# Fewer K, Q, V buffers, and the order of transposes, masks and states, in a fused retention and hard-swish MLP kernel

## The chip, the cores and the metric

The kernel runs on one core of a Trainium2 chip. The metric is the device time of one execution in microseconds (us); the time of a kernel is the median of its runs. Engines are named as the profile names them: PE is TensorE's matrix multiplication and PEld its weight load, DVE is VectorE, ACT is ScalarE, POOL is GpSimd, SP is SyncE. POOL and SP issue the transfers between memory and chip.

## What is computed

The inputs q, k, v have 8 batches, 8 heads, 576 positions and 64 elements per head, in float32. A retention layer without softmax is followed by two matrix products with an activation between them:

```
scores = (q @ k^T) / sqrt(64)                        # per batch and head
Dmat   = gamma_h ** (i - j) where i >= j, else 0     # gamma_h = 1 - 2**(-5-h)
x      = ((scores * Dmat) @ v), heads side by side   # 4608 tokens x 512
h      = x @ w_in                                    # 512 x 2048
out    = (h * clip(h + 3, 0, 6) / 6) @ w_out         # 2048 x 512, float32
```

## The kernel before

All matrix work is in float16 with sums in float32. Each sequence of 576 is cut into four pieces of 128 positions; the 64 positions that are left of two batches make a "rest" piece together. The 36 pieces, in the order of `pieces`, fill the columns of `xt16`, and 512 columns are a block (`MBLK`), so there are nine blocks. Block 0 is made of the pieces 0 to 3, block 1 of 4 to 7, block 2 of 8 to 11; the blocks 3, 5 and 7 need five new pieces, a rest piece first, the blocks 4 and 6 need four, and block 8 needs one.

A piece c goes through these steps:

- `load(c)`: K into the tile `kn`, Q and V into the two halves of `qv`, issued by POOL, which also turns float32 into float16. `kn` and `qv` have nine buffers each. A load can be issued when the last reader of its buffer is done.
- Transposes: Q (scaled by powers of gamma) and K are needed with the head's elements on the partitions, in the tile `qk`. For the first pieces this is done by PE and copied out of PSUM by ACT (`transposes_early`, tiles `trk` and `trq`; the diagonal matrices `dq` scale Q within the transposing product). Piece 4 has `transposes`, eight transposing products and one copy by DVE. From piece 8 on, SP issues two DMA transposes (`transposes_by_dma`), and DVE scales Q and V together in between (`vs`, L306); the transpose of Q waits for that.
- `scores`: eight products, then a mask by DVE gives `at`. `inter` multiplies Q by the state that the pieces before have left (`tbd`), `intra` multiplies `at` by V, both into the tile `o`; ACT copies `o` into `xt16`. `update_mm` and `update_state` make the next state. The pieces 0 to 3 do the latter in `state_early`, with a product by the unit matrix that adds the old state, and a scaling by DVE.

The MLP works by blocks. `g1(kb, fc)` is one of 16 units of GEMM1: four products of 128x512 into one of the four PSUM banks `ph`, then ACT (`u`, L416) and DVE (`gt`, L417) make the activation. `g2` is a quarter of a GEMM2 output tile `pout`: four products; after the fourth quarter ACT copies it to `osb` and SP stores it. Nothing plans at run time: the scheduler is manual, every engine takes its instructions in the order in which the program writes them. `put(units, steps)` writes GEMM units in order and hangs steps of the attention of the next block behind units by their number. In GEMM2 of block kb the attention of block kb+1 is done in the steps numbered -1, 7 and 12 (or -1, 3, 7 and 11 with five pieces), and `ahead` starts the transposes of block kb+2.

Before the first GEMM1 the pieces 0 to 3 are worked through alone, with products of zeros (`warm`) in gaps of PE. There, `make_mask` has POOL make the triangular mask between two loads. After GEMM2 of block 0, piece 7 is not done yet, so GEMM1 of block 1 begins by columns (`g1_columns`): first the columns 0 to 255 of four banks, then the third and the fourth 128 columns of all four.

The loads of GEMM1's weights (`load_win`), of the pieces and of GEMM2's weights (`load_wout`) stand in one order on POOL: pieces 0 to 3, `win` in five parts, piece 4, `wout` in four parts, pieces 5, 6, 7, then the others as `load_until` names them.

Of the kernel before, what the change touches and what calls it, by code (L numbers as in the profile page):

```python
# [17 lines left out]
def kernel(  # L18
# [64 lines left out]
    BY_PE = 8  # L83

    def load(c, behind_q=None):
        kn = nat.tile([P, H, D], FP16, tag="kn", bufs=9, name=f"kn_{c}")
        qv = nat.tile([P, 2, H, D], FP16, tag="qv", bufs=9, name=f"qv_{c}")
        loaded[c] = {"kn": kn, "qv": qv, "q16": qv[:, 0]}
        for dst, src in ((kn, k), (qv[:, 0], q), (qv[:, 1], v)):
            for p0, b, s0, n in pieces[c][3]:  # L90
                nc.gpsimd.dma_start(dst[p0:p0 + n],  # L91
                                    src[b, :, s0:s0 + n, :].rearrange("h s d -> s h d"))
            if src is q and behind_q is not None:
                behind_q()
# [6 lines left out]
    def load_wout(c0, c1):  # L101
# [4 lines left out]
    tcol = const.tile([P, 1], FP32)  # L106
    nc.gpsimd.iota(tcol, pattern=[[0, 1]], base=HALF, channel_multiplier=-1,
                   allow_small_or_imprecise_dtypes=True)
    zeros = const.tile([P, MBLK], FP16)
# [9 lines left out]

    mask_wide = const.tile([P, P + 1], FP16)  # L120
    nc.vector.memset(mask_wide, 1.0)

    def make_mask():
        nc.gpsimd.affine_select(out=mask_wide, in_=mask_wide, compare_op=ALU.is_ge, fill=0.0,
                                base=-1, pattern=[[1, P + 1]], channel_multiplier=-1)

    load(0, make_mask)
    mask01 = mask_wide[:, 1:P + 1]
    ident16 = const.tile([P, P], FP16)
    nc.vector.tensor_tensor(out=ident16, in0=mask01, in1=mask_wide[:, 0:P], op=ALU.subtract)  # L130
    lgc = const.tile([P, NPAIR], FP32)
    for p in range(NPAIR):
# [4 lines left out]
    gc = const.tile([P, 2, NPAIR], FP32)  # L137
    gfull = const.tile([P, NPAIR, P], FP32)
    nc.vector.memset(gfull, 0.0)

    tl = const.tile([P, H], FP32)
    nc.vector.tensor_scalar(out=tl, in0=lnr, scalar1=tcol[:, 0:1], scalar2=None, op0=ALU.mult)
    gv = const.tile([P, H], FP32)
    nc.scalar.activation(gv, tl, ACTF.Exp, bias=cb[:, 1:2])
    gq = const.tile([P, H], FP32)
    nc.scalar.activation(gq, tl, ACTF.Exp, scale=-1.0)

    dq = const.tile([P, H, P], FP16)
    nc.vector.tensor_tensor(out=dq, in0=ident16[:, None, :].to_broadcast([P, H, P]),
                            in1=gq[:, :, None].to_broadcast([P, H, P]), op=ALU.mult)  # L150
    nc.scalar.activation(gc[:, 0], lgc, ACTF.Exp, scale=float(P))
    nc.scalar.activation(gc[:, 1], lgc, ACTF.Exp, scale=float(HALF))
    nc.scalar.copy(gfull[0:HALF, :, 0:D],
                   gc[0:HALF, 0, :, None].to_broadcast([HALF, NPAIR, D]))
    nc.scalar.copy(gfull[HALF:P, :, D:2 * D],
                   gc[HALF:P, 0, :, None].to_broadcast([HALF, NPAIR, D]))
    gqv = const.tile([P, 2, H, D], FP16)
    nc.scalar.copy(gqv[:, 1], gv[:, :, None].to_broadcast([P, H, D]))
    nc.scalar.copy(gqv[:, 0], gq[:, :, None].to_broadcast([P, H, D]))
# [40 lines left out]
    def scale_v(c):  # L200
        vs = work.tile([P, 2, H, D], FP16, tag="vs", bufs=6, name=f"vs_{c}")
        st[c] = {"vs": vs[:, 1]}
        nc.vector.tensor_tensor(out=vs[:, 1], in0=loaded[c]["qv"][:, 1], in1=gqv[:, 1],
                                op=ALU.mult)

    def transposes_early(c, alone=True):
        kn, q16 = loaded[c]["kn"], loaded[c]["q16"]
        qk = work.tile([P, 2, NPAIR, P], FP16, tag="qk", bufs=6, name=f"qk_{c}")
        st[c]["qk"] = qk
        pk = psum.tile([P, NPAIR, P], FP16, tag="ph", bufs=4, name=f"trk_{c}")  # L210
        for p in range(NPAIR):
            nc.tensor.transpose(pk[:, p, :], kn[:, 2 * p:2 * p + 2, :], ident16)
        nc.scalar.copy(qk[:, 1], pk)
        if c == 0:
            warm(6, MBLK)
        elif alone:
            warm(8, P)
        pq = psum.tile([P, NPAIR, P], FP32, tag="ph", bufs=4, name=f"trq_{c}")
        for p in range(NPAIR):
            for h2 in range(2):  # L220
                r = slice(h2 * HALF, h2 * HALF + HALF)
                nc.tensor.matmul(pq[r, p, :], q16[:, 2 * p + h2, :], dq[:, 2 * p + h2, :],
                                 start=(p == 0), stop=(p == NPAIR - 1), skip_group_check=True)
        nc.scalar.copy(qk[:, 0], pq)  # L224
        if c == 0:
            warm(8, P)
# [54 lines left out]
    def scale(c):  # L281
        vs = work.tile([P, 2, H, D], FP16, tag="vs", bufs=6, name=f"vs_{c}")
        st[c] = {"qs": vs[:, 0], "vs": vs[:, 1]}
        nc.vector.tensor_tensor(out=vs, in0=loaded[c]["qv"], in1=gqv, op=ALU.mult)

    def transposes(c):
        kn = loaded[c]["kn"]
        qk = work.tile([P, 2, NPAIR, P], FP16, tag="qk", bufs=6, name=f"qk_{c}")
        st[c]["qk"] = qk
        ps = psum.tile([P, 2, NPAIR, P], FP16, tag="tu", name=f"tr_{c}")  # L290
        for i, src in ((1, kn), (0, st[c]["qs"])):
            for p in range(NPAIR):
                nc.tensor.transpose(ps[:, i, p, :], src[:, 2 * p:2 * p + 2, :], ident16)
        nc.vector.tensor_copy(qk, ps)

    def transposes_by_dma(c):
        qv, kn = loaded[c]["qv"], loaded[c]["kn"]
        qk = work.tile([P, 2, NPAIR, P], FP16, tag="qk", bufs=6, name=f"qk_{c}")
        vs = work.tile([P, 2, H, D], FP16, tag="vs", bufs=6, name=f"vs_{c}")
        st[c] = {"qk": qk, "vs": vs[:, 1]}  # L300

        def transpose(which, src):
            nc.sync.dma_start_transpose(qk[:, which], src.rearrange("s h d -> s (h d)"))

        transpose(1, kn)
        nc.vector.tensor_tensor(out=vs, in0=qv, in1=gqv, op=ALU.mult)  # L306
        transpose(0, vs[:, 0])
# [36 lines left out]
    def intra(c):  # L344
# [8 lines left out]
        nc.scalar.copy(xt16[:, :, g0:g0 + P], o)  # L353
# [18 lines left out]
    def update_state(c):  # L372
# [21 lines left out]
        nc.scalar.copy(tbd[new][0:HALF, :, 0:D], ts[0:HALF])  # L394
        nc.scalar.copy(tbd[new][HALF:P, :, D:2 * D], ts[HALF:P])  # L395
# [32 lines left out]
    def g1_columns(kb, banks, cols):  # L428

        t0 = kb * MBLK  # L430
        for fc, ph in enumerate(banks):
            for dmc in range(NCC):
                nc.tensor.matmul(ph[:, cols], win16[:, dmc, P * fc:P * fc + P],
                                 xt16[:, dmc, t0 + cols.start:t0 + cols.stop],
                                 start=(cols.start == 0 and dmc == 0),
                                 stop=(cols.stop == MBLK and dmc == NCC - 1),
                                 skip_group_check=True)
                if dmc == NCC - 1 and cols.stop == MBLK:
                    g1_act(kb, ph, fc)
# [10 lines left out]
    def store(kb, mc, cols, src):  # L450
# [3 lines left out]
        else:  # L454
            for i in range(2):
                r0 = (2 * mc + i) * S + MAIN
                nc.sync.dma_start(out[r0:r0 + HALF, cols], src[i * HALF:i * HALF + HALF])
# [38 lines left out]
    load(4)  # L496
    for i in range(4):
        load_wout(4 * i, 4 * i + 4)
    for c in (5, 6, 7):
        load(c)  # L500
# [7 lines left out]
    scale_v(0)  # L508
    for c in range(EARLY):
        transposes_early(c)  # L510
        if c > 0:
            inter(c - 1)
            intra(c - 1)
        if c < EARLY - 1:
            scores(c)
            run_later(9)
            state_early(c)
            run_later(9)
            scale_v(c + 1)
        else:  # L520
            scores_last(c)
            state_early(c)
            out_last(c)

# [6 lines left out]
    def early(c):  # L531
        scale_v(c)
        transposes_early(c, False)

    def second_half(c):
        inter(c)
        finish(c)

    def ahead(c):
        if c < NP:  # L540
            load_until(c + 4)
            transposes_by_dma(c)
# [22 lines left out]
    def step(ended, begun):  # L565
# [10 lines left out]
        for c in begun:  # L576
            run_later(1)
# [18 lines left out]
    def gemm1(kb, steps):  # L596
# [7 lines left out]
    gemm1(0, {12: [(scale, 4)]})  # L604
    order = [(mc, part) for part in range(4) for mc in range(3)] + [(3, part) for part in range(4)]
    put([unit2(0, mc, part) for mc, part in order],
        {0: [(transposes, 4)], 2: [(scores, 4)], 4: [(second_half, 4)],
         8: [(make_mask_rest,)], 10: [(early, 5)], 11: [(scores, 5)], 12: [(early, 6)],
         13: [(second_half, 5), (scores, 6)], 14: [(early, 7)],
# [4 lines left out]
    g1_columns(1, banks, slice(0, 2 * P))  # L614
    second_half(7)
    g1_columns(1, banks, slice(2 * P, 3 * P))
    ahead(8)
    g1_columns(1, banks, slice(3 * P, MBLK))
# [3 lines left out]
    gemm1(1, {2: [(ahead, 9)], 5: [(ahead, 10)], 8: [(ahead, 11)]})  # L622
    AT = {1: (-1, 7), 4: (-1, 7, 12), 5: (-1, 3, 7, 11)}
    for kb in range(1, NMB - 1):
# [5 lines left out]
        for c in mine[4:]:  # L630
            steps.setdefault(2, []).append((ahead, c))
        for c, j in zip(next_[:4], (12, 13, 14, 15)):
# [38 lines left out]
```

## Time and profile before

| | |
|---|---|
| runs before, median (lowest to highest) | 310.78 us (310.72 to 311.31), 3 runs |
| profiled execution | 311.39 us, of which the span of its instructions is 309.6 us |
| PE busy | 299.5 us (97% of the span), 2286 products |
| DVE, ACT busy | 185.8 us (60%), 173.6 us (56%) |
| POOL busy | 108.0 us (35%), 135 instructions |
| transfers issued by POOL (queue q0) | 117264 packets, 18.36 MB |
| transfers issued by SP (queue q1) | 35872 packets, 16.79 MB |

The span is the time from the first to the last instruction of one execution under the profiler. Times within it are counted from its start. A row of the timeline has start, duration, engine, line, operation, output and inputs, and how long the engine had been idle, with what ended that. Products overlap: a 128x512 product is shown with some 380 ns and the next starts some 216 ns after it, so the distance of two starts is the cost of one, not its shown duration.

### The profile page before, as it was taken

What the parts mean: (1) busy time and instruction counts of PE and PEld (TensorE: products, weight loads), DVE (VectorE), ACT (ScalarE), POOL (GpSimd) and SP (SyncE); (2) the same over time, 40 slices, a digit from 0 to 9 for tenths busy, and PEclk for the clock granted to TensorE, in tenths of its full rate; (3) what the DMA queues carried; (4) which work ended last, traced back from release to release, by engine and by line L of the source; (5) the groups of instructions that cost most, each with busy time, mean ns of one, the idle gap of its engine ahead of it and who ended that gap; (6) DMA issues with size and microseconds to landing.
All of it is one profiled execution on the core that took longest, in us unless ns stands there. A gap on an engine that the chain in (4) does not pass through costs nothing.

```text
span 309.6 us, 5856 instructions
## 1 busy us (share of the span) xinstructions
PE 299.5 (97%) x2286; PEld 152.6 (49%) x2286; DVE 185.8 (60%) x310; ACT 173.6 (56%) x298; POOL 108.0 (35%) x135
## 2 busy tenths in 40 slices
PE   8889999899999999999999999999999999999994
PEld 3644446544544554445544644455445544444443
DVE  4758715796737882885478737856688357207600
ACT  4657356773457554854574737644765467227611
POOL 8974378696735390045353720130000000000000
PEclk9999999999999999999999999999999999999999
DMA  9999999999999999539998996094423230010033
GB/s 65 145 197 190 204 156 211 168 140 156 191 174 170 114 171 163 118 24 154 146 166 74 140 184 138 17 123 69 104 51 53 83 55 0 34 70 34 1 70 68
DMA packets 153164, 35.52 MB, mean 115 GB/s; under 512 B 143792, under 2 KB 148656, under 8 KB 153136
## 3 DMA queue, kind: packets, MB, share of 16 engines
q0 software_dynamic: 117264, 18.36, 82.9%
q1 hardware_dynamic: 35872, 16.79, 27.6%
q8 instruction: 18, 0.29, 0.4%
q14 instruction: 10, 0.08, 0.1%
HBM read 36.70 MB, written 9.44 MB: 149 GB/s over the span
## 4 chain that ended last, share of the span: by engine, by line
PE 76%; DMA 16%; POOL 6%; issue 1%; DVE 0%; ACT 0%; POOLq 0%
PE pout L467 35%; PE ph L409 31%; DMA wout<-in_moe_w_out_dram 5%; POOL qv L91 4%; DMA win<-in_moe_w_in_dram 3%; DMA qv<-in_v_dram 3%; PE o L349 3%; DMA kn<-in_k_dram 3%; DMA qk<-vs 2%; POOL kn L91 2%; PE o L338 2%; PE sc L316 2%; PE u L367 1%; PE pout L480 1%; PE sc L552 1%
## 5 line engine op out<-in xcount | busy, mean ns | idle before, releaser
L417 DVE SCALAR_TENSOR_TENSOR gt<-u,ph 128x512 f16<-128x512 f32 x144 | 98.1, 687 | 69.0 <-ACT u L416 68.3
L467 PE MATMUL pout<-wout,gt 128*128 128x512 f16 x560 | 126.6, 380 | 0.0
L409 PE MATMUL ph<-xt,win 128*128 128x512 f16 x560 | 122.3, 379 | 1.4 <-DVE gt L417 1.4
L416 ACT ACTIVATE u<-ph,cb 128x512 f32<-128x512 f32 x144 | 98.5, 687 | 25.9 <-PE ph L409 25.4
L409 PEld LDWEIGHTS <-win 128*128 128x128 f16 x560 | 54.7, 98 | 67.3 <-issue 1.6
L467 PEld LDWEIGHTS <-gt 128*128 128x128 f16 x560 | 52.3, 98 | 60.8
L91 POOL DMA_DIRECT2D kn<-in_k_dram x40 | 34.4, 861 | 80.9 <-PE u L367 59.2
L471 ACT COPY osb<-pout 128x512 f32<-128x512 f32 x35 | 20.5, 585 | 48.1 <-PE pout L467 47.8
L91 POOL DMA_DIRECT2D qv<-in_q_dram x40 | 34.2, 858 | 7.4 <-DMA wout<-in_moe_w_out_dram 3.0
L320 DVE TENSOR_TENSOR at<-sc,mask_wide 128x1024 f16<-128x1024 f32 x19 | 23.2, 1223 | 22.4 <-PE sc L316 22.4
L91 POOL DMA_DIRECT2D qv<-in_v_dram x40 | 34.6, 868 | 3.2 <-DMA wout<-in_moe_w_out_dram 1.7
L394 ACT COPY tbd<-ts 64x256 f16<-64x256 f16 x28 | 11.3, 405 | 34.1 <-DVE ts L384 17.2
L353 ACT CAST xt<-o 128x512 f16<-128x512 f32 x35 | 19.3, 588 | 10.9 <-PE o L349 10.7
L306 DVE TENSOR_TENSOR vs<-qv,gqv 128x1024 f16<-128x1024 f16 x28 | 17.9, 684 | 0.0
L560 DVE TENSOR_TENSOR at<-sc,mask_wide 128x512 f16<-128x512 f32 x24 | 15.4, 681 | 0.0
L349 PE MATMUL o<-at,vs 128*64 128x128 f16 x280 | 12.2, 223 | 0.0
L395 ACT COPY tbd<-ts 64x256 f16<-64x256 f16 x28 | 11.2, 401 | 0.4
L383 DVE TENSOR_TENSOR ta<-u,ts 128x256 f32<-128x256 f32 x21 | 8.7, 416 | 3.6 <-PE u L367 3.6
L316 PE MATMUL sc<-qk 64*128 64x128 f16 x184 | 9.1, 218 | 1.2 <-ACT qk L224 1.1
L338 PEld LDWEIGHTS <-tbd 128*128 128x128 f16 x124 | 7.9, 98 | 4.5
L384 DVE TENSOR_TENSOR ts<-ta,gc 128x256 f16<-128x256 f32 x21 | 8.9, 425 | 1.7
L349 PEld LDWEIGHTS <-vs 128*64 128x64 f16 x280 | 8.6, 109 | 2.6 <-issue 0.4
(73 smaller groups left out, 120.1 us busy)
## 6 DMA issues: line engine op xcount, KB each, us to landing
out_dram<-osb SPq DMA_DIRECT2D x32, 256.0 KB, 3.5
kn<-in_k_dram POOLq DMA_DIRECT2D x32, 128.0 KB, 6.2
qv<-in_q_dram POOLq DMA_DIRECT2D x32, 128.0 KB, 6.3
qv<-in_v_dram POOLq DMA_DIRECT2D x32, 128.0 KB, 6.5
wout<-in_moe_w_out_dram POOLq DMA_DIRECT2D x4, 512.0 KB, 15.2
win<-in_moe_w_in_dram POOLq DMA_DIRECT2D x3, 512.0 KB, 10.1
out_dram<-osb SPq DMA_DIRECT2D x6, 128.0 KB, 2.3
win<-in_moe_w_in_dram POOLq DMA_DIRECT2D x2, 256.0 KB, 6.2
```

Of the source, the lines that this page charges most:

```text
L91: nc.gpsimd.dma_start(dst[p0:p0 + n], src[b, :, s0:s0 + n, :].rearrange("h s d -> s h d"))
L306: nc.vector.tensor_tensor(out=vs, in0=qv, in1=gqv, op=ALU.mult)
L316: nc.tensor.matmul(sc[:, h2, p, :], qk[r, 1, p, :], qk[r, 0, p, :], start=True, stop=True)
L320: later.append(lambda: nc.vector.tensor_tensor(out=at.rearrange("t a b s -> t (a b) s"), in0=sc.rearrange("t a b s -> t (a b) s"), in1=mas ...
L349: nc.tensor.matmul(o[r, p, :], vs[:, 2 * p + h2, :], at[:, h2, p, :], start=(st[c]["first"] and p == 0), stop=(p == NPAIR - 1), skip_group ...
L353: nc.scalar.copy(xt16[:, :, g0:g0 + P], o)
L409: nc.tensor.matmul(ph, win16[:, dmc, P * fc:P * fc + P], xt16[:, dmc, t0:t0 + MBLK], start=(dmc == 0), stop=(dmc == NCC - 1))
L416: nc.scalar.activation(u, ph, ACTF.Relu, bias=cb[:, 0:1], scale=1.0 / 6.0)
L417: nc.vector.scalar_tensor_tensor(out=gts[kb][:, fc, :], in0=u, scalar=1.0, in1=ph, op0=ALU.min, op1=ALU.mult)
L467: nc.tensor.matmul(pout, gt[:, fc, P * mc:P * mc + P], wout16[:, fc, :], start=(fc == 0), stop=(fc == NFC - 1))
L471: nc.scalar.copy(osb, pout)
L560: nc.vector.tensor_tensor(out=at[:, h2], in0=banks[h2], in1=mask[:, None, :].to_broadcast([P, NPAIR, P]), op=ALU.mult)
```

## The change

It has these parts:

1. `kn` and `qv` have five buffers, not nine. `load(c + 5)` is written where the reading of piece c ends (behind `update_mm`), where before `load_until(c + 4)` stood in `ahead(c)`. In POOL's order piece 4 now follows the second of four `wout` parts.
2. The DMA transposes of all pieces of a block are written at the last units of the GEMM2 ahead: behind the units 12 to 15 for four pieces, 11 to 15 for five. Before, the fifth piece's stood at unit 2 of the next GEMM2. For the pieces 8 to 11 the transposes of K and of Q are written apart.
3. First pieces: POOL's iota fills 128x129, and DVE makes the mask from it; the constants are made in another order; gamma fills of ACT come later (`fill_gfull`, `fill_gq`). Of the 47 products of zeros, nine of 128x512 stay at the start, and 2, 2, 1, 1 and 1 of 128x512 stand in place of six of 128x512 and 32 of 128x128. `inter` and `intra` of the piece before stand between K's and Q's transposes, their copy to `xt16` behind. For piece 3, ACT copies Q in two halves.
4. `state_early(3)`, that is four products of 128x128, one of 128x512 and a DVE scaling, moves from ahead of GEMM1 of block 0 to behind its unit 5.
5. Piece 4 is transposed as the pieces 5 to 7 are, behind unit 4 of GEMM2, where before `transposes` stood behind unit 0.
6. In the columns of block 1, the third and fourth parts of the four banks alternate, DVE scales piece 8 before the state of piece 7, and ACT's two copies of that state come behind the fifth `u`.
7. In the last block, where each output tile is stored by two transfers, ACT issues the second.

```diff
-        kn = nat.tile([P, H, D], FP16, tag="kn", bufs=9, name=f"kn_{c}")
-        qv = nat.tile([P, 2, H, D], FP16, tag="qv", bufs=9, name=f"qv_{c}")
+        kn = nat.tile([P, H, D], FP16, tag="kn", bufs=NBUF, name=f"kn_{c}")
+        qv = nat.tile([P, 2, H, D], FP16, tag="qv", bufs=NBUF, name=f"qv_{c}")
...
-    nc.gpsimd.iota(tcol, pattern=[[0, 1]], base=HALF, channel_multiplier=-1,
+    wide = const.tile([P, P + 1], FP32)
+    nc.gpsimd.iota(wide, pattern=[[1, P + 1]], base=-1, channel_multiplier=-1,
...
-    def make_mask():
-        nc.gpsimd.affine_select(out=mask_wide, in_=mask_wide, compare_op=ALU.is_ge, fill=0.0,
-                                base=-1, pattern=[[1, P + 1]], channel_multiplier=-1)
-    load(0, make_mask)
+    nc.vector.tensor_scalar(out=mask_wide, in0=wide, scalar1=0.0, scalar2=None, op0=ALU.is_ge)
...
+        behind = between() if between is not None else None
         pq = psum.tile([P, NPAIR, P], FP32, tag="ph", bufs=4, name=f"trq_{c}")
...
-        nc.scalar.copy(qk[:, 0], pq)
-        if c == 0:
-            warm(8, P)
+        if c == EARLY - 1:
+            for p in (0, 2):
+                nc.scalar.copy(qk[:, 0, p:p + 2], pq[:, p:p + 2])
+        else:
+            nc.scalar.copy(qk[:, 0], pq)
+        if behind is not None:
+            behind()
...
+    def transpose_k(c):
+        nc.sync.dma_start_transpose(qk_of(c)[:, 1], loaded[c]["kn"].rearrange("s h d -> s (h d)"))
+
+    def transpose_q(c):
         vs = work.tile([P, 2, H, D], FP16, tag="vs", bufs=6, name=f"vs_{c}")
...
+        nc.sync.dma_start_transpose(st[c]["qk"][:, 0], vs[:, 0].rearrange("s h d -> s (h d)"))
...
-                nc.sync.dma_start(out[r0:r0 + HALF, cols], src[i * HALF:i * HALF + HALF])
+                queue = nc.scalar if i else nc.sync
+                queue.dma_start(out[r0:r0 + HALF, cols], src[i * HALF:i * HALF + HALF])
...
-    load(4)
     for i in range(4):
+        if i == 2:
+            load(4)
         load_wout(4 * i, 4 * i + 4)
...
     scale_v(0)
+    transposes_early(0, lambda: warm(2, MBLK))
+    fill_gfull()
+    warm(2, MBLK)
     for c in range(EARLY):
-        transposes_early(c)
         if c > 0:
-            inter(c - 1)
-            intra(c - 1)
+            def last_one():
+                warm(1, MBLK)
+                inter(c - 1)
+                return intra(c - 1, copy_later=True)
+            transposes_early(c, last_one)
...
             scores_last(c)
-            state_early(c)
             out_last(c)
...
     def ahead(c):
-        if c < NP:
-            load_until(c + 4)
-            transposes_by_dma(c)
+        transpose_k(c)
+        transpose_q(c)
...
         update_mm(begun)
         for c in begun:
+            load_until(c + NBUF)
             run_later(1)
             update_state(c)
...
-    gemm1(0, {12: [(scale, 4)]})
+    gemm1(0, {5: [(state_early, EARLY - 1), (load_until, 8)], 9: [(fill_gq,)]})
...
-        {0: [(transposes, 4)], 2: [(scores, 4)], 4: [(second_half, 4)],
-         8: [(make_mask_rest,)], 10: [(early, 5)], 11: [(scores, 5)], 12: [(early, 6)],
-         13: [(second_half, 5), (scores, 6)], 14: [(early, 7)],
+        {4: [(early, 4, "tu")], 6: [(scores, 4)], 8: [(second_half, 4), (make_mask_rest,)],
+         10: [(early, 5)], 11: [(scores, 5)], 12: [(early, 6)],
+         13: [(second_half, 5), (scores, 6)], 14: [(early, 7), (transpose_k, 8)],
...
-    g1_columns(1, banks, slice(0, 2 * P))
-    second_half(7)
-    g1_columns(1, banks, slice(2 * P, 3 * P))
-    ahead(8)
-    g1_columns(1, banks, slice(3 * P, MBLK))
+    for fc in range(4):
+        g1_columns(1, fc, banks[fc], slice(0, 2 * P))
+    transpose_q(8)
+    inter(7)
+    intra(7)
+    update_mm([7])
+    load_until(7 + NBUF)
+    update_state(7, copies_later=True)
+    third, fourth = slice(2 * P, 3 * P), slice(3 * P, MBLK)
+    for fc, cols in ((0, third), (1, third), (0, fourth), (2, third), (1, fourth), (3, third),
+                     (2, fourth), (3, fourth)):
+        g1_columns(1, fc, banks[fc], cols)
...
-    gemm1(1, {2: [(ahead, 9)], 5: [(ahead, 10)], 8: [(ahead, 11)]})
+    gemm1(1, {0: [(transpose_k, 9)], 1: [(transpose_q, 9), (transpose_k, 10)],
+              5: [(transpose_q, 10), (transpose_k, 11)], 9: [(transpose_q, 11)]})
...
-        for c in mine[4:]:
-            steps.setdefault(2, []).append((ahead, c))
-        for c, j in zip(next_[:4], (12, 13, 14, 15)):
+        for j, c in enumerate(next_, start=16 - len(next_)):
             steps.setdefault(j, []).append((ahead, c))
```

## Prediction, made before the change was run

> **What bounds the kernel now.** I read the page's busy table first, then PE's waits, then the timeline at each wait.
>
> ```profile
> PE 299.5 (97%) x2286; PEld 152.6 (49%) x2286; DVE 185.8 (60%) x310; ACT 173.6 (56%) x298; POOL 108.0 (35%) x135
> ```
>
> PE is the bound. A change gains only where PE stands still, before its first GEMM product and after its last; it loses where it gives PE more products inside the GEMMs. The waits of PE say where it stands:
>
> ```profile
> PE ph L409 <- DVE gt L417: 1.4, 1, 1.4
> PE trq L222 <- DMA qv<-in_q_dram: 0.9, 1, 0.9
> PE sc L552 <- DMA qk<-vs: 0.6, 1, 0.6
> PE o L258 <- DVE at L240: 0.3, 1, 0.3
> ```
>
> The second and fourth lie in the first pieces, the first in the columns of block 1, the third at the start of GEMM2 of block 1. After that there is none. PE's timeline for the first pieces' end:
>
> ```profile
> 14.97 0.61 PE L175 MATMUL warm<-zeros 128*128 128x128 f16 x8
> 16.44 0.41 PE L222 MATMUL trq<-dq,qv 128*64 128x128 f16 x8 [0.86 <-DMA qv<-in_q_dram]
> ...
> 17.53 0.40 PE L237 MATMUL sc<-qk 64*128 64x128 f16 x8
> 17.86 0.40 PE L269 MATMUL u<-vs,kn 128*128 128x128 f16 x4
> 18.10 0.38 PE L273 MATMUL u<-tbd,ident 128*128 128x512 f16 x1
> 18.31 0.39 PE L252 MATMUL o<-qk,tbd 128*128 128x128 f16 x4
> ...
> 19.55 0.82 PE L409 MATMUL ph<-xt,win 128*128 128x512 f16 x3
> ```
>
> From 19.55 to 305.3 PE runs with 2.1 us of waits; from there to 309.6 the last stores land. The sum below is against the profiled execution, 311.39 us; the median of the runs is 0.61 us lower.
>
> **1. First pieces, -0.5 us.** The end hangs on Q of piece 3: landed 16.39, then `trq` 16.44, ACT's copy 0.58, scores 17.53, two masks of 0.65 each from 17.97 to 19.26, products 19.31, GEMM1 19.55. Two halves of the copy (`xt` by L261, 128x256, takes 0.37) let the scores begin 0.21 earlier. Q of piece 3 itself was late: the transfers before it landed every 0.85 us up to 13.95, it came 2.4 us later. In the packet record a 16,384-byte packet of queue q8 (instructions) starts at 14.34 and takes 0.945 us, just when PE has issued 259 weight loads and products; the page counts 18 such packets for 4,572 of these, one for 254. With 31 zero products fewer, PE's 256th instruction is within piece 3's `trq`, after Q is there. Then what binds is DVE: each piece costs it mask 1.22, state 0.68 and V 0.42, the mask of piece 2 ends at 15.65 as before, `intra(2)` runs to 16.05, `trq` follows, the first half of the copy ends at 16.9, masks run from 17.35 to 18.65 and GEMM1 starts at 18.95: -0.6. If Q stays late, -0.2. The larger iota stands before the first load on POOL; 0.13 us for one column and 0.32 for the removed mask on 129 columns put it near 0.3, and it replaces that mask in the queue, so V of piece 0 and all later loads move by 0.1 at most (a 0.6 us iota would delay them by 0.2). Ends: +0.2 and -0.7; I take -0.5. The removed zero products cost nothing if the PE clock holds: the one wait of 0.86 us above left later products at 216 ns.
>
> The Trainium skill, "Runtime: NRT & Kernel Launch", section "Instruction fetch mechanics", says that a block of 256 instructions is fetched at a time and that crossing is mostly hidden. The count above agrees with the block; the lateness of Q speaks against "hidden". By the rule this part would be -0.2 and the total 0.3 us higher.
>
> **2. State of piece 3 into GEMM1, +0.45 us.** Before, its products took PE from 17.86 to 18.31 while the masks were running, free. Behind unit 5 they stand in a full PE: 18.31 - 17.86. Its DVE scaling (0.68) was beside GEMM1 before as well (22.97). `fill_gq` puts 0.61 us on ACT there; ACT needs 0.69 of each unit's 0.86 us and may lag 0.9 before a bank is missed: nothing. Ends 0.2 and 0.6.
>
> **3. Piece 4 transposed by `early`, +0.2 us.** Piece 5 shows it: 44.32 to 44.99, 0.67 us of PE; the old `transposes` took 34.23 to 34.68. The load of piece 4 moves behind two `wout` parts of 2.5 us each: from 30.47 to some 35.5, needed at 37.5; the third `wout` part lands at 37.8, as before, needed at 38.9. Nothing if both hold; a lag would be PE's time one to one. Ends 0.1 and 1.0.
>
> **4. Columns of block 1, -0.7 us.** Before, ACT and DVE were late:
>
> ```profile
> 57.17 0.40 ACT L394 COPY tbd<-ts 64x256 f16<-64x256 f16 x1 [0.53 <-DVE ts L384]
> 57.59 0.40 ACT L395 COPY tbd<-ts 64x256 f16<-64x256 f16 x1
> 58.01 3.21 ACT L416 ACTIVATE u<-ph,cb 128x512 f32<-128x512 f32 x5
> ```
>
> The first bank was ready at 58.0 and free at 59.42, when DVE had made its `gt`. Now the first bank's fourth part is the third group; it needs the copy of piece 7 to `xt16` (to 56.63), so it ends at 56.9, `u` runs to 57.8, `gt` to 58.55, and the next unit starts at 58.6, not 59.47. The two copies, now behind the fifth `u`, and `vs` of piece 9 behind the sixth `gt` push one bank by 0.2 us. -0.87 + 0.2. Ends -0.9 and -0.3.
>
> **5. Q of piece 9, -0.6 us.** Its transpose was issued at 64.30, behind `vs` at 63.58, and landed at 70.83, 6.5 us on, because POOL's loads of the pieces 12 to 16 filled the same queues. Now `vs` stands one unit earlier, and with five buffers piece 13 cannot be loaded before `update_mm` of piece 8, at 69. The loads 10 and 11 wait for pieces 5 and 6 (49.7 and 53.2 us, issued before at 48.39 and 50.98), but the transfer engines have 6 us of work queued then, so they land about when they did, 58.5 and 62.4; DVE needs them at 65 and 68. What is late next would be Q of piece 11, needed at 76. Ends -0.64 and 0.
>
> **6. Last stores, -0.5 us.** The last two are issued by SP at 305.73 and 306.25 and land at 307.65 and 308.31. ACT, free after its copy, issues the second at about 305.8. Ends -0.66 and 0.
>
> **7. Late loads of the five-piece blocks, +0.4 us.** This is the wait that the change adds. With four pieces in work and five next, the loads of the last two are released at unit 7 of GEMM2 and DVE scales the last behind unit 15. GEMM2 of block 3 before has just such a burst:
>
> ```profile
> 144.77 0.88 POOL L91 DMA_DIRECT2D kn<-in_k_dram  x1 [3.65 <-PE u L367]
> ...
> 149.10 0.94 POOL L91 DMA_DIRECT2D qv<-in_v_dram  x1
> ...
> 154.06 0.69 DVE L417 SCALAR_TENSOR_TENSOR gt<-u,ph 128x512 f16<-128x512 f32 x1 [4.20 <-ACT u L416]
> ```
>
> There nobody waited for it; now DVE would, with GEMM1's `gt` queued behind. GEMM1 starts at 152.27, its fifth unit needs the first bank at 155.73; back by `gt` 0.69 and `vs` 0.66, the last load must land by 154.33. Before it landed at 156.20, with an instruction packet of 0.965 us at 152.2 among its last packets. PE's 54 instructions fewer move that packet some 6 us on; most of the burst's packets were through by 154. So 154.0 to 154.8, or 0 to 0.5 us a block, three blocks (3, 5, 7). Ends 0 and 3 x 1.87 = 5.6; I take 0.4. In the other blocks the loads are released at unit 3 or earlier.
>
> The sum: -0.5 + 0.45 + 0.2 - 0.7 - 0.6 - 0.5 + 0.4 = -1.25; the profiled execution comes to 310.1, the median to 309.5.
>
> **The rivals.** *Late loads win (slower).* If the burst lands as it did before, each of the three blocks loses 1.87 us: -1.65 + 5.6 = +4, 314.7. For it: the trace's own landing. Against: its last packets came after an instruction packet that moves. It turns the sign from 0.55 us a block, a landing at 154.9. 20%.
> *The stalls stay (no change).* ACT and DVE pace the columns whatever the order, Q of piece 3 and of piece 9 stay late: -0.2 + 0.65 - 0.3 - 0.5 + 0.4 = 0, about 310.8. 13%.
> *The clock falls.* With 16 zero products for 47, PE's share in the first pieces sinks; the first nine are 0.43 us apart, twice the later 0.216. Eight GEMM1 products at that distance cost 1.7 us, so +0.45, 311.2. Against: PE keeps over three quarters busy there. 4%.
> My forecast has the rest, 63%.
>
> **Range and chances.** 0.2% is 0.62 us, about what a measurement can tell from no change. All good ends give -2.6, 308.2, of which 308.5 leaves out the last step; the bad side reaches into the late loads, to two thirds of 1.87 us in each block: 312.9, cut at 312.3 where 2 in 10 are outside. Range 308.5 to 312.3; the forecast's own, 308.5 to 310.3. Faster by over 0.2%: 0.64; within: 0.13; slower: 0.23.
>
> **What would show it.** Right: GEMM1's first product near 19.0; a wait of PE on `gt` in the columns of some 0.5; none at `sc` L552; a last landing 0.5 us nearer to PE's end. Wrong: DVE waiting for V in front of `gt` at the ends of the GEMM2s of the blocks 1, 3 and 5, with PE waiting for a bank 3.5 us later; products at 0.43 us after 8 us; PE waiting for `wout` or piece 4 in GEMM2 of block 0.

## The result, and the profile after

The changed kernel takes 313.26 us (median of 6 runs, 312.02 to 314.02) against 310.66 us before (6 runs, 309.95 to 311.31). The ratio is 1.0083, with a 95% interval of 1.0054 to 1.0112: it is slower, by 2.6 us, where 1.25 less was forecast. The profiled execution is 312.65 us with a span of 310.4 (before 311.39 and 309.6), so from trace to trace the loss is 1.26: 0.80 in the span and 0.46 outside it. The rest lies between traces and medians: the span before is 0.8 above the median of 63 executions of that kernel (308.8), the span after 0.55 below the median of its six (310.95).

The page of the changed kernel, busy table and two groups (in a group's row: busy time and mean ns, then the idle time before and what ended most of it):

```profile
PE 298.0 (96%) x2259; PEld 150.8 (49%) x2259; DVE 184.8 (60%) x309; ACT 174.2 (56%) x301; POOL 107.8 (35%) x134
...
L408 PE MATMUL ph<-xt,win 128*128 128x512 f16 x560 | 123.0, 379 | 2.6 <-DVE gt L416 2.6
...
L292 DVE TENSOR_TENSOR vs<-qv,gqv 128x1024 f16<-128x1024 f16 x28 | 18.4, 686 | 20.0 <-DMA qv<-in_v_dram 12.9
```

PE has 1.5 us less to do and stands still elsewhere: the GEMM1 products wait 2.6 us for `gt`, and DVE's scaling `vs` waits 12.9 us for V's load. PE's waits of the changed kernel (sum, times, longest):

```profile
PE ph L408 <- DVE gt L416: 2.6, 4, 0.9
...
PE sc L302 <- ACT qk L229: 1.3, 2, 0.7
...
PE trq L223 <- DMA qv<-in_q_dram: 1.0, 1, 1.0
...
PE o L263 <- DVE at L245: 0.5, 2, 0.3
PE sc L242 <- ACT qk L227: 0.5, 1, 0.5
```

Before, `gt` was waited for once, 1.4 us in the columns; now four times. The wait for Q's transpose (`qk<-vs`, 0.6) is gone. Three of the four `gt` waits are new, at the start of GEMM1 of the blocks 2, 4 and 6. The chain of waits of the changed kernel (start, duration, what) passes through the same load each time:

```profile
83.33 6.48 DMA qv<-in_v_dram
91.34 10.52 PE ph L408 x48
...
148.39 5.90 DMA qv<-in_v_dram
155.82 10.52 PE ph L408 x48
...
212.86 6.43 DMA qv<-in_v_dram
220.82 10.52 PE ph L408 x48
```

The timeline around the first of them shows who stands behind whom:

```profile
83.33 0.93 POOL L91 DMA_DIRECT2D qv<-in_v_dram  x1
...
86.80 3.62 PE L408 MATMUL ph<-xt,win 128*128 128x512 f16 x16
...
90.00 0.69 DVE L292 TENSOR_TENSOR vs<-qv,gqv 128x1024 f16<-128x1024 f16 x1 [3.67 <-DMA qv<-in_v_dram]
...
90.61 2.47 DVE L416 SCALAR_TENSOR_TENSOR gt<-u,ph 128x512 f16<-128x512 f32 x4
...
91.34 1.89 PE L408 MATMUL ph<-xt,win 128*128 128x512 f16 x8 [0.93 <-DVE gt L416]
```

V of the fifth piece is issued at 83.33 and lands at 89.81. DVE stands 3.67 us in front of `vs`, though ACT's `u` of the first unit was done at 88.55. The four `gt` that had piled up follow without a pause, and PE, whose four banks are full after 16 products, waits 0.93 us. The timeline at the two places where the forecast had put a gain, the end of the first pieces and the columns:

```profile
15.86 0.42 PE L223 MATMUL trq<-dq,qv 128*64 128x128 f16 x8
...
18.92 1.25 PE L408 MATMUL ph<-xt,win 128*128 128x512 f16 x5
...
57.21 3.21 ACT L415 ACTIVATE u<-ph,cb 128x512 f32<-128x512 f32 x5 [0.53 <-PE ph L431]
...
58.68 1.67 PE L408 MATMUL ph<-xt,win 128*128 128x512 f16 x7 [0.44 <-DVE gt L416]
```

GEMM1 starts 0.63 us earlier, and in the columns `u` follows PE where it followed two copies of ACT, so PE waits 0.44 instead of 1.44 us. Stage by stage, from one trace to the other:

| what | before | after | effect on what follows, us |
|---|---|---|---|
| GEMM1 of block 0 starts | 19.55 | 18.92 | -0.63 |
| its length (state of piece 3) | 13.82 | 14.26 | +0.44 |
| GEMM2 of block 0 (piece 4) | 20.15 | 20.39 | +0.24 |
| columns, up to the next whole unit | 5.95 | 5.11 | -0.84 |
| from there to GEMM2 of block 1 | 12.20 | 11.49 | -0.71 |
| GEMM1 of the blocks 2, 4, 6 | 14.71, 14.71, 14.70 | 15.79, 15.22, 15.74 | +2.63 |
| last product's start | 305.03 | 306.16 | +1.13, the sum |
| from it to the last landing | 3.29 | 2.90 | -0.39 |

The first five rows give -1.50, and the three waits turn it round.

### The profile page after: what moved, and what is told of

Same layout as the page of the kernel before. It is cut to its first block, busy times and chain, and to the rows that moved or that the text cites. A ratio compares the mean times of both kernels' runs of the same rounds, so it can differ in the third digit from the quotient of the medians.

```text
span 310.4 us, 5817 instructions
## 1 busy us (share of the span) xinstructions
PE 298.0 (96%) x2259; PEld 150.8 (49%) x2259; DVE 184.8 (60%) x309; ACT 174.2 (56%) x301; POOL 107.8 (35%) x134
## 4 chain that ended last, share of the span: by engine, by line
PE 54%; issue 18%; DMA 13%; POOL 10%; DVE 3%; ACT 1%; SPq 0%; POOLq 0%; DVEq 0%
PE ph L408 24%; PE pout L466 22%; DMA qv<-in_v_dram 6%; POOL qv L91 5%; POOL kn L91 4%; DMA qv<-in_q_dram 4%; DMA qk<-kn 3%; PE o L335 2%; PE sc L302 2%; DVE at L306 1%; PE pout L479 1%; PE o L324 1%; DVE vs L292 1%; PE u L359 1%; PE trq L223 1%
## 5 line engine op out<-in xcount | busy, mean ns | idle before, releaser
L292 DVE TENSOR_TENSOR vs<-qv,gqv 128x1024 f16<-128x1024 f16 x28 | 18.4, 686 | 20.0 <-DMA qv<-in_v_dram 12.9
```

## The experiments

Each ratio is against the kernel before, timed beside it on the same chip; that kernel's median was 310.46, 310.62 or 310.92 us there, so medians of different experiments can differ by half a microsecond for that alone.

**Which wait: six buffers.** If the late V is the loss, one more buffer releases the loads of the burst one piece earlier.

```diff
-    NBUF = 5
+    NBUF = 6
```

> The changed kernel with six buffers of K, Q, V in place of five, nothing else. Theory A (late loads: DVE waits for V of the fifth piece of blocks 3, 5 and 7 with GEMM1's gt queued behind it): the load of that piece is still released at unit 7, but alone, three loads of 0.87 us earlier, so it lands about 2.6 us sooner; the three PE waits on gt (0.93, 0.36, 0.87 us idle; 2.6 us of shift in all) are gone, the profiled span falls from 310.4 to about 307.8 and the median to about 310.7 minus 0.0 to 0.5, that is no slower than before. Theory B (the loss is in what varies between executions, a clock that falls with fewer zeros or time outside the span): the median stays 2 to 3 us above before.

Measured: 310.00 (12 runs, 309.32 to 311.87), ratio 0.999 (0.9974 to 1.0007), span 307.7. Of PE's `gt` waits only the one in the columns is left:

```profile
PE ph L408 <- DVE gt L416: 0.4, 1, 0.4
```

The last product starts at 303.42, 2.74 earlier than in the changed kernel. In the trace the late load is the whole loss. Without it the rest of the change is worth 0.46 us in the median, not 1.65, and the interval reaches past no gain at all.

**Late transfer, or the order on DVE?** Five buffers stay, and only the fifth piece's `ahead` (the scaling and two transposes) goes from the end of GEMM2 into unit 5 of the next GEMM1; the other four pieces' stand one unit later, behind the units 12 to 15. The loads are released and issued as in the changed kernel.

```diff
-        for j, c in enumerate(next_, start=16 - len(next_)):
+        for j, c in enumerate(next_[:4], start=16 - len(next_[:4])):
...
-        gemm1(kb + 1, {})
+        gemm1(kb + 1, {5: [(ahead, c) for c in next_[4:]]})
```

> The changed kernel with five buffers, but the scaling and the two transposes of the fifth piece of blocks 3, 5, 7 (and of the one piece of none other) are written behind unit 5 of the next GEMM1, not behind unit 15 of the GEMM2. The loads are as late as in the changed kernel. Theory A, in the form that the order on DVE does the harm: the loads land where they did (89.8, 154.3, 219.3) but nobody waits, the three PE waits are gone and the span is about 307.8. If instead the transfers themselves (their contention) slowed PE, the span stays near 310.4. Theory B: median unchanged, about 313.

Measured: 310.16 (12 runs, 309.24 to 313.01), ratio 0.9994 (0.9973 to 1.0015), span 307.7, last product at 303.51. The timeline of this kernel at the same place:

```profile
83.33 0.92 POOL L91 DMA_DIRECT2D qv<-in_v_dram  x1
...
86.79 6.42 PE L408 MATMUL ph<-xt,win 128*128 128x512 f16 x29
...
88.58 0.69 DVE L416 SCALAR_TENSOR_TENSOR gt<-u,ph 128x512 f16<-128x512 f32 x1 [2.36 <-ACT u L415]
```

The load is issued at 83.33 and lands at 89.80, as before this edit (89.81). But `gt` runs at 88.58, right behind `u`, and PE goes through 29 products instead of stopping after 16. So the transfer's time costs nothing in itself; it costs because a DVE instruction that waits for it stands ahead of `gt` in DVE's order.

**Five buffers alone.** The kernel before with five buffers and loads released behind the reading, all else as it was:

```diff
-        kn = nat.tile([P, H, D], FP16, tag="kn", bufs=9, name=f"kn_{c}")
-        qv = nat.tile([P, 2, H, D], FP16, tag="qv", bufs=9, name=f"qv_{c}")
+        kn = nat.tile([P, H, D], FP16, tag="kn", bufs=5, name=f"kn_{c}")
+        qv = nat.tile([P, 2, H, D], FP16, tag="qv", bufs=5, name=f"qv_{c}")
...
-            load_until(c + 4)
...
+            load_until(c + 5)
```

> The kernel before with five buffers, and the loads released where the reading of piece c ends, as in the change; all else as before, so the fifth piece's scaling stands behind unit 2 of the next GEMM2 and not ahead of GEMM1's gt. Theory A: five buffers alone do no harm, because nothing that PE needs soon is queued behind a late load: no wait of PE on gt at the starts of the GEMM1s, median within 0.6 us of before, possibly 0.3 to 0.6 better by the missing wait for Q of piece 9. Rival (five buffers are too few whatever the order): 1.5 to 3 us slower.

Measured: 309.82 (12 runs, 309.55 to 310.64), ratio 0.998 (0.9967 to 0.9994), span 308.0. V of the same piece lands even later, at 91.08 (issued 83.23), and nobody waits, because the fifth piece's `ahead` stands at unit 2 of the next GEMM2. Fewer buffers alone are a small gain; they cost only together with the earlier place of the fifth piece. The waits and the first pieces' end on PE in this kernel (two views):

```profile
PE ph L409 <- DVE gt L417: 1.4, 1, 1.4
```

```profile
15.50 0.41 PE L222 MATMUL trq<-dq,qv 128*64 128x128 f16 x8
...
18.61 1.69 PE L409 MATMUL ph<-xt,win 128*128 128x512 f16 x7
```

The columns' wait is still 1.4, and the wait at `sc` L552 is gone. And GEMM1 starts at 18.61 with the old order of the first pieces: Q of piece 3 landed at 15.30 here, 1.1 us earlier than in the trace the prediction was made from. The new order of the first pieces starts at 18.92 in the changed kernel. What step 1 gained, it gained on an execution in which Q was late.

**Was that execution a rare one?** One profile more of the kernel before, unchanged:

> The kernel before, unchanged, for a second trace. The first trace's span was 309.6 us; the spans of 23 further executions of it have a median near 308.8. Theory C (the trace that the prediction summed from was a slow execution: Q of piece 3, landed at 16.39, and the wait of 0.64 us for Q of piece 9 are not there in a usual one): Q of piece 3 lands near 15, GEMM1 starts 0.3 to 0.7 us earlier, or the 0.64 us wait is absent, and the span is near 308.8. Rival: the same waits as in the first trace, span 309.3 to 309.7.

Its span is 309.8, Q of piece 3 landed at 16.56, late again, and GEMM1 started at 19.71. So this execution does not show the other case. Its wait for Q of piece 9 is 0.23 us, with another of 0.30 us for a transpose later in the same GEMM2, where the first trace had 0.64 and none. The spans of the 63 executions of the kernel before run from 307.8 to 309.8, with a median of 308.8, and both traces lie at the upper end; that most executions start GEMM1 earlier fits these spans but no trace of that kernel shows it.

**The second last store back on SP:**

```diff
-                queue = nc.scalar if i else nc.sync
+                queue = nc.sync
```

> The changed kernel with the second store of each last output tile issued by SP again, not by ACT. If the second issuer saves what the trace shows, the last landing is 0.4 us later after PE's end (3.3 us, not 2.9) and the median is 0.4 us above the changed kernel's, 313.6. Theory B1 (a second queue costs time outside the span, where the changed kernel shows 1.8 to 2.8 us against 1.8 before): the time outside the span goes back to 1.8 in all runs and the median falls by up to 0.5 us.

Measured: 313.34 (6 runs, 311.93 to 313.70), ratio 1.0083 (1.0062 to 1.0105). The last landing comes 3.30 us behind the last product's start, against 2.90 with the store on ACT: 0.4 us, which the runs' spread hides. The time outside the span goes from 1.73 to 2.75 here too, so the store on ACT does not cause it.

**The zero products back** (4 for 2, 2 for 1, and 2 more behind Q's transposes of the pieces 1 and 2):

```diff
-    transposes_early(0, lambda: warm(2, MBLK))
+    transposes_early(0, lambda: warm(4, MBLK))
...
-                warm(1, MBLK)
+                warm(2, MBLK)
...
+            if c < EARLY - 1:
+                warm(2, MBLK)
```

> The changed kernel with more zero products between those of the first pieces (4 for 2 behind the first transposes, 2 for 1 ahead of each inter, and 2 more of 128x512 behind each Q transpose of pieces 1 and 2, where PE waits 0.7 us for ACT). Theory B2 (in some executions the clock falls, as the mean clocks of 0.995 and 0.999 in two of six runs hint): all mean clocks are 1.000, the runs near 314 vanish and the median falls from 313.3 to about 312.5, with the three waits on gt unchanged. Theory A alone: the spread and the median stay as they were, 312 to 314; GEMM1 starts at 18.9 to 19.2.

Measured: 315.63 (6 runs, 313.70 to 316.68), ratio 1.0152 (1.0122 to 1.0183): against what was expected, slower still. Of the 4.5 us that its span is longer than the changed kernel's (314.9 for 310.4), 2.5 lie in the waits for `gt`, which were expected to stay as they were:

```profile
PE ph L408 <- DVE gt L416: 5.1, 4, 2.5
```

Behind the first burst PE waits 2.49 us instead of 0.93. V takes 8.05 us from its issue to its landing there (85.26 to 93.31), and a 16,384-byte packet of the instruction queue starts in between, at 89.82; in the changed kernel that packet starts at 90.12, behind the landing. The nine traces of the changed kernel and its variants agree: in the bursts in GEMM2 of the blocks 1 and 3, the last load takes 5.9 to 6.9 us in the 13 cases in which no such packet starts between its issue and its landing, and 7.3 to 8.1 us in the five in which one does. In the four traces with the old places of the transposes (the kernel before twice, five buffers alone, and the last experiment below) such bursts always had one, with 6.6 to 7.9 us in six cases.

The other 1.9 us lie at the start. The stretches ahead of, in and behind GEMM1's first products (start to end, length, busy time and count of PE, PEld, DVE, ACT and POOL, the granted clock, DMA share and GB/s):

```profile
15.00:18.77 3.77, 2.01 (x37) 1.55 (x36) 2.01 (x5) 1.47 (x4) 2.76 (x4) 1.00 1.35 179
18.77:22.18 3.41, 3.15 (x15) 1.15 (x13) 0.41 (x1) 0.74 (x2) 2.09 (x3) 0.50 1.24 205
22.18:30.00 7.82, 7.82 (x41) 3.69 (x40) 5.59 (x9) 6.07 (x9) 2.38 (x3) 1.00 1.24 207
```

From 18.77, just ahead of GEMM1, the granted clock is 0.50 for 3.41 us. In the stretch ahead PE was busy for 2.01 of 3.77 us, since V of piece 3 landed only at 17.53 (15.68 in the changed kernel) and PE waited 1.10 us for a mask. GEMM1 starts at 19.59, 0.67 us later than in the changed kernel, and is 1.27 us longer (15.53 for 14.26). The Trainium skill, "TensorE: Matmul & The Clock Gate", Part 1, states that the gate halves the clock after an idle window of about 3.4 us; the fall above lasts as long, 3.41 us, but it comes after 3.41 us in which PE was busy for 1.65 us, about half. In the other 12 traces PE's busy share is at least 0.61 in any 3.41 us between 5 us and GEMM1, and the clock does not fall. That is one fall in one trace: it fits a late V as the cause, and no run moved V alone. Four of the six executions have a mean clock of 0.993 to 0.995, against one of six of the changed kernel, so more zeros did not hold the clock up.

**Zeros only where PE was idle** (on six buffers, two behind Q's transposes of the pieces 1 to 3):

```diff
                 return intra(c - 1, copy_later=True)
             transposes_early(c, last_one)
+            warm(2, MBLK)
```

> The changed kernel with six buffers, and two zero products of 128x512 behind the Q transposes of pieces 1, 2 and 3, where PE waits 0.67, 0.67 and 0.46 us for ACT. Theory E (the clock falls for one stretch of 3.4 us in some executions, mean clock 0.993 to 0.995, because PE idles too much in the first pieces): no execution shows a mean clock under 0.996, the spans over 309 vanish, median near 309.8. Rival (what decides is a late V or Q of piece 3, not these gaps): one execution in five still shows 0.993 to 0.995.

Measured: 309.67 (12 runs, 309.20 to 311.57), ratio 0.9977 (0.9961 to 0.9993). One of 12 executions still has a lower mean clock (0.994, span 309.8 for a median of 307.8); with six buffers alone there were 2 of 12, and 4 of 12 with the fifth piece later. That these zeros prevent the fall is not shown. None of the 63 executions of the kernel before, nor of the 18 with the old first pieces, has a mean clock of 0.995 or less.

**The time outside the span.** It is 1.65 to 1.86 in the kernel before, 1.8 to 2.8 in the changed one. In the trace of the changed kernel the last 16,384-byte packet of the instruction queue starts at 311.5, after the span's end; before it started at 298.5. Ten one-column products of zeros, each with a weight load, in the columns' gap, on six buffers, move it back into the kernel:

```diff
+    w = psum.tile([P, 2, NPAIR, P], FP32, tag="sc", name="page")
+    for _ in range(10):
+        nc.tensor.matmul(w[:, 0, 0, 0:1], zeros[:, 0:P], zeros[:, 0:1], start=True, stop=True)
```

> The changed kernel with six buffers, and ten zero products of one column in the 0.44 us in which PE waits in the columns of block 1: 20 more PE instructions. Theory D (with 54 PE instructions fewer the last 16 KB instruction packet falls behind the last product, at 309.5 to 312.8 in the traces, and the program's end waits for it): the packet comes ahead of the last landing, and the time outside the span, 1.8 to 2.9 us with six buffers, is 1.65 to 1.9 in all executions as in the kernel before; the median falls by 0.2 us to about 309.8. Rival: the time outside the span varies as before, median 310.0.

Measured: 309.78 (12 runs, 309.48 to 312.44), ratio 0.9985 (0.9966 to 1.0004). The packet starts at 300.31, and the time outside is 1.77 to 1.92 in all 12, for 1.77 to 2.91 without. So up to about 1 us of some executions hung on it; the medians differ by 0.2 us. The same products move another instruction packet into the burst of GEMM2 of block 1 (from 89.75, behind V's landing, to 88.70), and V takes 8.02 us there instead of 6.36; nobody waits for that load with six buffers.

**The state of piece 3 back ahead of GEMM1** (on six buffers):

```diff
+            state_early(c)
...
-    gemm1(0, {5: [(state_early, EARLY - 1), (load_until, 8)], 9: [(fill_gq,)]})
+    gemm1(0, {5: [(load_until, 8)], 9: [(fill_gq,)]})
```

> The changed kernel with six buffers, and the state of piece 3 made ahead of GEMM1 again, between the scores and the last products of piece 3. The prediction's step 2 says that the move cost 0.45 us of a full PE: GEMM2 of block 0 starts 0.4 to 0.45 us earlier after GEMM1's start, which itself stays at 18.7 to 19.1, since PE waits there for DVE's masks; the span falls from 307.7 to 307.2, the median from 310.0 to 309.5. Rival: the products come between the scores and the last products and delay GEMM1's start by the same 0.45; nothing is won.

Measured: 309.01 (6 runs, 308.93 to 309.73), ratio 0.995 (0.9931 to 0.997). GEMM1 starts at 18.77 and takes 13.81 instead of 14.26: the 0.45 of step 2. The median falls by 0.99, more than that; the two were not timed beside each other, and all six executions have a mean clock of at least 0.998, which may be the rest. With the zeros behind Q's transposes as well:

> As state_ahead, and two zero products of 128x512 behind the Q transposes of pieces 1 to 3 (12 PE instructions more, so the last instruction packet comes ahead of the end). If both add up: time outside the span 1.75 to 1.95, median 309.2 to 309.3. If PE's idle time in the last 3.4 us ahead of GEMM1 decides on the clock, now at its smallest, no execution has a mean clock under 0.996; rival: one in ten still has.

309.03 (6 runs, 308.86 to 309.36), ratio 0.9946 (0.9926 to 0.9966). These two beat both kernels.

**The old first pieces with the good parts:** five buffers alone, plus the alternating columns and the last store on ACT.

```diff
-    def update_state(c):
+    def update_state(c, copies_later=False):
...
+    for fc, cols in ((0, third), (1, third), (0, fourth), (2, third), (1, fourth), (3, third),
+                     (2, fourth), (3, fourth)):
+        g1_columns(1, fc, banks[fc], cols)
...
+                queue = nc.scalar if i else nc.sync
```

> The kernel before with five buffers, as five_alone, and two more parts of the change: the alternating columns of block 1 (with the state copies behind the fifth u) and the second of the last stores by ACT. The first pieces, piece 4 and the places of ahead are those of the kernel before. If the parts add up: columns -0.85, last landing -0.4 against five_alone, so the span is near 306.8 and the median near 308.6, better than both kernels, and no execution has a clock under 0.996, which would tie the falls of the clock to the new order of the first pieces. Rival: the columns' gain is taken back by the wait for Q of piece 9 (up to 0.64), median 309.2; or the clock falls here too, in one execution of ten.

Measured: 309.09 (6 runs, 308.88 to 309.32), ratio 0.9946 (0.9927 to 0.9964), span 307.1. Two of PE's waits in this kernel:

```profile
PE ph L416 <- DVE gt L424: 0.4, 1, 0.4
PE sc L559 <- DMA qk<-vs: 0.3, 1, 0.3
```

The columns' wait falls from 1.4 to 0.4, but with K and Q of piece 9 transposed together, as in the kernel before, GEMM2 of block 1 waits again for Q, 0.3 us. It equals the best versions with the new first pieces, which therefore gain nothing that these times can tell.

## Why the prediction was wrong

The rival *late loads win* named what happened; the forecast sized it too small and took it for the less likely case.

**Step 7 is the step that failed.** It took 0 to 0.5 us a block, 0.4 in all; measured were 1.08, 0.51 and 1.04, 2.6 in all. The mechanism was the one forecast: DVE waits for V, `gt` stands behind it, PE runs out of banks. The arithmetic from the landing to PE held to 0.14 us. By it GEMM1 may start 2.06 us ahead of the landing (154.33 - 152.27) at no cost (the subtraction as written gives 154.38; the 0.05 decides nothing). The landings at 89.81, 154.29 and 219.29, with GEMM1 at 86.80, 151.85 and 216.33, then cost 0.95, 0.38 and 0.90, and the stages grew by 0.13 to 0.14 more, since PE's next product came 1.53 us behind the landing and not 1.40. (The list of waits shows 0.93, 0.36 and 0.87, because it counts from a product's drawn end, some 0.16 us behind the time at which the next could have started.)

What was mis-sized is the last transfer. The prediction let it land 4.9 to 5.7 us after its issue (149.10, landing 154.0 to 154.8), because an instruction packet of 0.965 us would be out of the way. It is out of the way in all three bursts (one starts at 90.12, behind the landing, the others at 144.45 and 208.93, ahead of the issue), and V still takes 6.48, 5.90 and 6.43. So a packet in the way goes with a later landing, as the prediction argued (7.3 to 8.1 us with one in the changed kernel's variants, 5.9 to 6.9 without), but what is left without it was taken too low. The first load of the first burst took 3.6 us (79.00 to 82.59). In the same 6 us as the last one a store (83.48 to 87.89) and K's transpose (83.99 to 89.94) were in transfer; whether they are what the last loads wait for was not tested. The rival's price (1.87 a block) was twice what came, since in GEMM2 of block 3 V was issued 3.46 us ahead of GEMM1 instead of 3.17 and landed 1.2 us sooner after its issue (5.90 for 7.10). That no packet fell into a burst was luck of the count: with the zero products back one did, and that wait was 2.49 us.

**Step 1 was right on its trace, and open for the median.** GEMM1's first product came at 18.92, forecast 18.95. But the old order starts at 18.61 when Q is on time (five buffers alone); if most executions are like that, as the spans suggest and no trace of the kernel before shows, this term was about nothing for the median. With the new order Q lands between 14.65 and 15.04 in all nine traces, so it may have removed the lateness where that occurred. Nor is the packet that step 1 blamed shown as the cause: with five buffers alone a like packet starts at 14.2 and Q lands at 15.30, while in the trace before it starts at 14.34 and Q lands at 16.39.

**The steps 2 to 6 held.** State of piece 3 +0.44 (forecast +0.45), piece 4 +0.24 (+0.2), the columns -0.84 (-0.7), Q of piece 9 -0.71 (-0.6, most of it the wait of 0.64, which the second trace of the kernel before does not have at that size), last stores -0.39 (-0.5). Their sum with step 1's is -1.89, forecast -1.65.

**What no step held** is what the median also paid: the time outside the span, with the last instruction packet behind the last product, and the clock that now falls in some executions. The rival *the clock falls* had the second, but as a rule for all executions; it came in one of the six runs of the changed kernel (0.995, span 312.1), and its cause is settled no further than the one trace above. What spoke against it, that PE keeps over three quarters busy, did not hold ahead of GEMM1: 2.66 of 3.92 us in the changed kernel.

## What to carry to other kernels

An instruction that waits for a load should stand, on its in-order engine, behind the work that the busiest engine waits for; the same three loads cost 2.6 us in all or nothing, by that place. Size the landing of a burst's last transfer as a range from the bursts that traces show (here 5.9 to 8.1 us): the one burst known gave +5.6 us for the three blocks, a correction argued from one packet gave +0.4, and 2.6 came. Before a term of a sum is taken from one profiled wait, see whether the span of that execution is near the median of the runs or at their edge.

## What the runs showed that was not expected

- A kernel with 27 matmuls and as many weight loads fewer on PE moved its last 16,384-byte instruction packet behind its own end, and the time outside the span rose from at most 1.86 to as much as 2.8 us. The Trainium skill, "Runtime: NRT & Kernel Launch", section "Instruction fetch mechanics", calls the crossing of a block mostly hidden. Inside the kernel PE's lists of waits name none for instructions, which agrees; but a load in transfer beside such a packet landed later (8.02 us for 6.36), and at the kernel's end the packet made some executions longer.
- The clock falls once to 0.50 for 3.41 us just at GEMM1's start, after a stretch in which PE was busy 2.01 of 3.77 us. Executions with a lower mean clock (0.993 to 0.995) have spans 1.2 to 3.4 us above the median of their kernel, the one with the zero products back left aside, in which most are like that.
- In the first pieces Q or V of piece 3 lands late in some executions and not in others of nearly the same program: with the new first pieces V lands at 15.4 to 15.8 in five traces (15.68 in the changed kernel) and at 16.7 to 17.5 in four (16.88 with six buffers, 17.53 with more zeros). What decides it stays open.
